# Pairs 0 to 5 of an attention stage: rotation on the vector engine, transposed weights copied out by the scalar engine

## The chip, the cores and the metric

The kernel runs on one core of a Trainium2 chip. The metric is the device time of one execution in microseconds (us), the median of several runs. PE is TensorE, DVE is VectorE, ACT is ScalarE, POOL is GpSimd, SP is the engine whose queue issues the DMA transfers.

## The reference

Rotary attention over 4 batches, 8 heads, 576 positions and 64 dimensions, then two feed-forward blocks over the 2304 tokens (model width 512, hidden width 2048), all in float32:

```python
q_rot, k_rot = rotate(q), rotate(k)     # x1*cos - x2*sin, x1*sin + x2*cos
scores = scale * q_rot @ k_rot.T
scores = scores - max(scores)
attn = exp(scores); attn = attn / (sum(attn) + 1e-9)
x = attn @ v                            # laid out as 2304 x 512
h = x @ w_in                            # first block
g = where(h >= 1, h, where(h <= -1, 0, (h + 1) ** 2 / 4))
x = g @ w_out
g = s * relu(x @ w_in2) ** 2 + b        # second block
out = g @ w_out2
```

## The kernel before, in words

Two heads are handled together as a pair: 16 pairs, i = 0 to 15. To keep float32 accuracy, operands are split into a high part in the float32r type and a low part (the rest), and products are summed from both.

The rotation of a pair's q or k is `rope_pair` (line 240 onwards). The tile holds q (or k) twice, as it is and with its halves swapped, 576 columns each. It is multiplied by the table of cosines and sines (1152 elements per partition, L246) and the two halves are added (576 elements, L248). Where GpSimd does it, `pool_tt` (L86) cuts an operation into pieces of at most 300 elements. For q, `lay_q` (L261, L262) writes high and low parts stacked for the matmuls. For k, `lay_k` copies the high part by the scalar engine (L272, tile `kin`), subtracts it to get the low part (576 elements), and spreads both by six DMA transfers (L277, L278) into `kh` and `kz`. For pair 0 all of this is done in halves on DVE ahead of the loop.

The scores of a pair are made in nine units, k = 0 to 8: eight of 128 rows of one head (four of head 0, four of head 1) and one, k = 4, of the 64 last rows of both heads. A unit is (`qk`): matmuls into one of two score buffers `sc` in PSUM (L305), the row maximum `nm` by DVE straight out of PSUM (L307), and exponential with row sums by ACT (L312) into the tile `p` in SBUF. The score buffer is free for the next unit but one when the exponential is done.

Two units later (`tmain`) PE transposes `p` in four blocks of 128x128 into a PSUM bank `tp` (L327), which is copied to `pt` in SBUF (512 elements per partition): units of head 0 by ACT (L331), unit 4 by ACT (L329), units of head 1 by DVE (L333). The last 64 columns are gathered and transposed after units 4 and 8 (`trem`) and copied to `ptr` by DVE (L344), 384 and 256 elements. After units 4 and 8, `inverse` takes reciprocals of the sums (L365, L367, L369 on DVE, L371 on POOL), and two units further `finish` multiplies the weights by v (`av`, L353), transposes the reciprocals (`rm`), copies them by ACT (L383) and scales the result by DVE (L386) into `u`, which goes to DRAM.

Beside the pairs, weights of the feed-forward blocks are loaded and converted from their 64-bit form (`Slice.half`): ACT L126, four steps on DVE (L127 to L130), ACT L131, two steps on POOL (L86, tiles `wm` and `w`). From pair 5 on, matmuls of the first block on the batches already finished fill PE (`beside`, matmuls at L144).

One loop over n (the number of the unit, 9 for each pair) calls, in the order "qltaf", the units' scores, the loads and rotations, the transposes, the products with v and the filling. The rotation of pair i + 1 is called in pair i, q at k = 0 and k at k = 2:

```python
if k == 0:
    rope_pair(i + 1, "q", nc.gpsimd if i else nc.vector, nc.vector, None)
elif k == 2:
    rope_pair(i + 1, "k", nc.gpsimd, nc.gpsimd, [nc.gpsimd, nc.vector])
```

So before, pair 1's q is multiplied by DVE and all later ones by GpSimd; all adds for q are on DVE; everything for k from pair 1 on is on GpSimd. A scheduler then sets the order on each engine; it takes rotations as early as buffers allow (four tiles for q and k together), up to two pairs ahead. Each engine runs its instructions strictly in that order.

After the attention, the rest of the first block and the second block run as dense matmuls (`stage`).

Of the kernel before, what the change touches and what calls it, by code (L numbers as in the profile page):

```python
# [14 lines left out]
ALU = mybir.AluOpType  # L15
# [8 lines left out]
P = 128  # L24
# [28 lines left out]
N2A = 288  # L53
CAV = None
BF = 0
SPLITX = 1
N1 = 288

# [2 lines left out]
def kernel(ctx, tc, qq, kk, vv, tab, ww1, ww2, s, b, out):  # L61
    nc = tc.nc
# [12 lines left out]
    def pool_tt(out, in0, in1, op, dim=-1):  # L75

        n = out.shape[dim]
        free = 1
        for x in out.shape[1:]:
            free *= x  # L80
        k = min(n, -(-free // PW))
        for i in range(k):
            c = [slice(None)] * len(out.shape)
            c[dim] = slice(n * i // k, n * (i + 1) // k)
            c = tuple(c)
            nc.gpsimd.tensor_tensor(out=out[c], in0=in0[c], in1=in1[c], op=op)  # L86
# [112 lines left out]
    ps_s = pp.enter_context(tc.tile_pool(name="ps_s", bufs=2, space=PSUM))  # L199
    ps_b = pp.enter_context(tc.tile_pool(name="ps_b", bufs=4 - BF, space=PSUM))  # L200
    ps_f = pp.enter_context(tc.tile_pool(name="ps_f", bufs=BF, space=PSUM)) if BF else ps_b

    tab_sb = att.tile([P, 2, S], F32, name="tab_sb")

    def bank(name):
        return ps_b.tile([P, 512], F32, tag="bank", name=name)
# [6 lines left out]
    def load_qk(i, nm, pieces=WHOLE):  # L213
        bb, hp = divmod(i, NP)
        t = att2.tile([P, 2, S], F32, tag="qkin", name=f"{nm}in", bufs=QB)
        for c in pieces:
            nc.sync.dma_start(out=t[:, :, c], in_=(qq if nm == "q" else kk)[bb, hp, :, :, c])
        qk_in[nm, i] = t

    def load_v(i):  # L220
        bb, hp = divmod(i, NP)
        t = att2.tile([P, 5, 2, D], F32, tag="vin", name="vin", bufs=VB)
        nc.sync.dma_start(out=t, in_=vv[bb, hp])
        v_in[i] = t
# [15 lines left out]
    def rope_pair(i, nm, mul, add, lo_eng, pieces=WHOLE):  # L240

        t = qk_in.pop((nm, i))
        tt = {nc.gpsimd: pool_tt, nc.vector: nc.vector.tensor_tensor}
        last = None
        for c in pieces:
            tt[mul](out=t[:, :, c], in0=t[:, :, c], in1=tab_sb[:, :, c], op=ALU.mult)  # L246
            r = t[:, 1, c]
            tt[add](out=r, in0=t[:, 0, c], in1=r, op=ALU.add)  # L248
            last = (lay_q if nm == "q" else lay_k)(i, t, c, lo_eng)
        return last  # L250
# [13 lines left out]
    def lay_k(i, t, c, lo_engs):  # L264
        if c.start == 0:
            stacks["k", i] = att.tile([P, 2, S], F32R, tag="kh", name="kh", bufs=2), kz_t[i % 2]
        kh, kz = stacks["k", i]
        tt = {nc.gpsimd: pool_tt, nc.vector: nc.vector.tensor_tensor}
        r = t[:, 1, c]
        if i > 0:  # L270
            hi, lo = t[:, 0, c].bitcast(F32R), r.bitcast(F32R)
            nc.scalar.copy(hi, r)  # L272
            pool_tt(out=lo, in0=r, in1=t[:, 0, c], op=ALU.subtract)
            for j in range(2):
                own = SELF[j]
                for rows in SELF:
                    nc.sync.dma_start(out=kh[rows, j, c].bitcast(F32), in_=t[own, 0, c])  # L277
                m = nc.sync.dma_start(out=kz[own, j, c].bitcast(F32), in_=t[own, 1, c])  # L278
            return m.ins
        for j in range(2):  # L280
            own, other = SELF[j], SELF[1 - j]
            nc.scalar.copy(kh[own, j, c], r[own])
            m = nc.sync.dma_start(out=kh[other, j, c].bitcast(F32), in_=kh[own, j, c].bitcast(F32))
            tt[lo_engs[j]](out=kz[own, j, c], in0=r[own], in1=kh[own, j, c], op=ALU.subtract)
        return m.ins
# [4 lines left out]
    pt = {}  # L290
# [25 lines left out]
    def tmain(i, k):  # L316
        j, t = UNITS[k]
        g, o = (0, 256) if j is None else divmod(t * P, 256)
        if k in (0, 5):
            n = GROUPS[g][1]  # L320
            pt[g] = att.tile([P, 4, 2, n], F32, tag="pt", name="pt", bufs=TB)
            pt["r", g] = att.tile([P, 384], F32, tag="ptr", name="ptr", bufs=TB)
        tp = bank("tp")
        v = tp.rearrange("p (c w) -> p c w", c=4)
        p = p_t[i, t][:, (S + D) * (j == 0):]
        for c in range(4):
            nc.tensor.transpose(v[:, c, :], p[:, c * P:(c + 1) * P], ident)  # L327
        if j is None:
            nc.scalar.copy(pt[g][:, :, :, o:o + D], tp.rearrange("p (c j w) -> p c j w", c=4, j=2))  # L329
        elif j == 0:  # L330
            nc.scalar.copy(pt[g][:, :, 0, o:o + P], v)  # L331
        else:
            nc.vector.tensor_copy(pt[g][:, :, 1, o:o + P], v)  # L333

    def trem(i, g):

        tp = bank("tr")
        for n in range(2):
            nc.tensor.transpose(tp[:, n * P:(n + 1) * P], p_t.pop((i, 2 * g + n))[:, 512:640], ident)
        m = 256  # L340
        if g == 0:
            nc.tensor.transpose(tp[:, 256:384], p_t.pop((i, 4))[:, 512:640], ident)
            m = 384
        nc.vector.tensor_copy(pt["r", g][:, :m], tp[:, :m])  # L344

    def av(i, g):

# [104 lines left out]
    def convert():  # L452
        while pending:
            sl = pending.pop(0)
            if sl.made < 2:
                sl.half(wst, WB)
                break
# [20 lines left out]
    def do_load(n):  # L478
        if n < len(units):
            i, k = units[n]  # L480
            if i + 1 < NPAIR:
                if k == 0:
                    rope_pair(i + 1, "q", nc.gpsimd if i else nc.vector, nc.vector, None)
                elif k == 2:
                    rope_pair(i + 1, "k", nc.gpsimd, nc.gpsimd, [nc.gpsimd, nc.vector])
                elif k == 3:
                    load_v(i + 1)
                elif k in (4, 6) and i + 2 < NPAIR:
                    load_qk(i + 2, "q" if k == 4 else "k")

        if n in range(33, 51, 2) or n in range(70, 110, 4):
            with tc.issue_after(exps[n - 14]):
                convert()

    def do_t(n):
        if LT <= n < len(units) + LT:
            i, k = units[n - LT]
            tmain(i, k)
            if k in (4, 8):
                trem(i, k // 8)  # L500
                rbs[i, k // 8] = inverse(i, k // 8)
# [9 lines left out]
    def do_fill(n):  # L511
        if n < 48:
            return
        with tc.issue_after(exps[min(n, len(units)) - 4]):
            run_fill(0.85 if n < 90 else 0.98)

    acts = {"q": do_qk, "l": do_load, "t": do_t, "a": do_av, "f": do_fill}
    for n in range(len(units) + LA):
        with ExitStack() as st:
# [156 lines left out]
```

## Time and profile before

| what | value |
|---|---|
| median of 3 runs | 1170.19 us |
| lowest and highest of them | 1165.18 and 1172.96 us |
| the profiled execution | 1167.95 us |
| its span, first to last instruction | 1166.2 us |
| mean granted TensorE clock | 0.988 |
| PE busy | 1104.3 us (95%) |
| DVE busy | 604.2 us (52%) |
| ACT busy | 692.6 us (59%) |
| POOL busy | 563.5 us (48%) |
| last product of the attention scaled (L386) | 462.2 us from the start |

The span begins with the first instruction; times in rows are counted from there. Busy shares are means over stages of different kinds: the attention with little else (to some 150 us), the attention with fillings (to 462 us), and the dense stages. PEclk is the clock granted to TensorE, 1.00 for full speed; a PE busy at a lower clock does less in the same time. In a row of the timeline the square brackets hold how long the engine was idle before it and what ended that.

### The profile page before, as it was taken

The page shows a single profiled execution, that of the slowest core. Times are in us where ns is not written, and L with a number is a line of the kernel's source. Part 1 is how long each engine was busy: PE and PEld are TensorE (multiplying, and loading weights), DVE is VectorE, ACT ScalarE, POOL GpSimd, SP SyncE. Part 2 cuts the span into 40 slices and gives each one's busy share as a digit, 9 for nine tenths or more (in the row PEclk, how much of TensorE's full clock was granted, in tenths as well). Part 3 has the DMA queues.
Part 4 walks back from the last instruction along what each step waited for, and adds up shares of the span by engine and source line. Part 5 has one row for each costly group of instructions (what it writes and reads, how often), then busy time and mean ns, then how long its engine had stood idle before and what let it go on. Part 6 is the DMA issues. An engine that isn't in the chain of part 4 may idle for free.

```text
span 1166.2 us, 18826 instructions
## 1 busy us (share of the span) xinstructions
PE 1104.3 (95%) x6816; PEld 997.2 (86%) x6816; DVE 604.2 (52%) x1030; ACT 692.6 (59%) x1450; POOL 563.5 (48%) x748
## 2 busy tenths in 40 slices
PE   4988799889999999999999889999999999999998
PEld 3666688778889988998999889998888889988887
DVE  6788888886565553566655566554411111221221
ACT  4666667756666655666555455567665555555443
POOL 6977797774441101766688886556610110111000
PEclk9988899999999999999999999999999999999999
DMA  7655555554443311434345453434211210312220
GB/s 230 185 163 154 155 160 172 175 160 123 124 120 97 91 40 58 142 124 135 102 147 157 146 166 132 131 122 145 94 38 60 66 40 26 98 39 70 66 65 33
DMA packets 68573, 132.63 MB, mean 114 GB/s; under 512 B 8448, under 2 KB 46592, under 8 KB 68480
## 3 DMA queue, kind: packets, MB, share of 16 engines
q1 hardware_dynamic: 68480, 131.43, 37.0%
q8 instruction: 53, 0.87, 0.3%
q14 instruction: 40, 0.33, 0.1%
HBM read 91.29 MB, written 26.54 MB: 101 GB/s over the span
## 4 chain that ended last, share of the span: by engine, by line
PE 69%; POOL 9%; DVE 8%; DMA 5%; issue 4%; ACT 4%; SPq 1%; POOLq 0%; ACTq 0%; DVEq 0%
PE hps L144 23%; PE yps L590 8%; PE yps L591 8%; PE yps L589 8%; PE sc L305 6%; PE h L144 4%; PE av L353 4%; PE y L144 4%; PE tp L327 3%; POOL w L86 2%; POOL wm L86 2%; DMA xs<-xd 2%; POOL xl L86 2%; DVE nm L307 1%; ACT p L312 1%
## 5 line engine op out<-in xcount | busy, mean ns | idle before, releaser
L144 PE MATMUL hps<-xh,w 128*128 128x464 f32 (+5 forms) x1216 | 344.4, 349 | 0.9 <-POOL w L86 0.9
L86 POOL TENSOR_TENSOR xl<-xs,xh 128x232 fp32r<-128x232 f32 (+5 forms) x172 | 132.3, 793 | 270.9 <-ACT xh L90 270.7
L144 PEld LDWEIGHTS hps<-xh,w 128*128 128x128 f32 x1216 | 221.7, 188 | 16.1 <-POOL w L86 1.1
L589 PE MATMUL yps<-gh,w 128*128 128x464 f32 (+5 forms) x608 | 213.3, 351 | 4.6 <-ACT yo L596 4.2
L590 PE MATMUL yps<-gl,w 128*128 128x464 f32 (+5 forms) x608 | 212.7, 350 | 5.1 <-DVE gl L94 5.1
L591 PE MATMUL yps<-gh,w 128*128 128x464 f32 (+5 forms) x608 | 212.5, 350 | 0.0
L144 PE MATMUL hps<-xl,w 128*128 128x464 f32 (+5 forms) x608 | 211.5, 348 | 0.4 <-POOL xl L86 0.4
L94 DVE TENSOR_TENSOR gl<-ar,gh 128x464 fp32r<-128x464 f32 (+1 forms) x80 | 56.7, 708 | 266.9 <-ACT gh L90 266.8
L86 POOL TENSOR_TENSOR wm<-wm,w 128x256 f32<-128x256 f32 x128 | 114.5, 914 | 119.7 <-ACT w L131 61.1
L305 PE MATMUL sc<-kh,qs 128*128 128x288 f32 (+2 forms) x384 | 110.7, 323 | 44.6 <-ACT p L312 31.3
L307 DVE TENSOR_REDUCE nm<-sc 128x1 f32<-128x576 f32 x144 | 107.4, 751 | 62.7 <-PE sc L305 62.4
L589 PEld LDWEIGHTS yps<-gh,w 128*128 128x128 f32 x608 | 114.5, 188 | 14.4 <-ACT yo L596 6.0
L590 PEld LDWEIGHTS yps<-gl,w 128*128 128x128 f32 x608 | 114.6, 189 | 13.5 <-DVE gl L94 6.0
L312 ACT ACTIVATE p<-sc,nm 128x576 f32<-128x576 f32 x144 | 106.7, 743 | 29.6 <-DVE nm L307 28.8
L175 ACT ACTIVATE ar<-hps 128x464 f32<-128x464 f32 (+1 forms) x80 | 44.3, 554 | 129.8 <-PE hps L144 129.8
L144 PEld LDWEIGHTS hps<-xl,w 128*128 128x128 f32 x608 | 114.2, 188 | 8.3 <-POOL xl L86 0.7
L591 PEld LDWEIGHTS yps<-gh,w 128*128 128x128 f32 x608 | 114.6, 189 | 7.5
L305 PEld LDWEIGHTS sc<-kh,qs 128*128 128x128 f32 x384 | 71.4, 198 | 53.3 <-ACT p L312 38.6
L305 PE MATMUL sc<-kz,qs 128*128 128x288 f32 (+2 forms) x384 | 100.6, 298 | 0.0
L86 POOL TENSOR_TENSOR w<-wm,wa 128x256 fp32r<-128x256 f32 x128 | 99.7, 795 | 0.1
L94 DVE TENSOR_TENSOR gl<-ac,gh 128x288 fp32r<-128x288 f32 (+3 forms) x112 | 78.0, 696 | 35.0 <-ACT gh L90 33.5
L327 PE MATMUL tp<-ident,p 128*128 128x128 f32 x576 | 90.4, 281 | 0.0
(81 smaller groups left out, 1991.3 us busy)
## 6 DMA issues: line engine op xcount, KB each, us to landing
wraw<-in_ww SPq DMA_DIRECT2D x64, 512.0 KB, 3.8
kin<-in_k SPq DMA_DIRECT2D x15, 576.0 KB, 4.6
qin<-in_q SPq DMA_DIRECT2D x15, 576.0 KB, 4.0
kh<-kin SPq DMA_DIRECT2D x60, 144.0 KB, 2.6
xs<-y1d SPq DMA_DIRECT2D x32, 232.0 KB, 2.5
xs<-xd SPq DMA_DIRECT2D x44, 144.0 KB, 2.3
yd<-ys SPq DMA_DIRECT2D x40, 144.0 KB, 2.2
vin<-in_v SPq DMA_DIRECT2D x16, 320.0 KB, 3.0
```

Source lines behind the costliest of these rows:

```text
L86: nc.gpsimd.tensor_tensor(out=out[c], in0=in0[c], in1=in1[c], op=op)
L94: tt(out=dst_lo, in0=src, in1=dst_hi, op=ALU.subtract)
L144: m = nc.tensor.matmul(out_ps, l, r, start=(i == 0), stop=(i == n - 1))
L175: nc.scalar.activation(r, h, AF.Relu)
L305: nc.tensor.matmul(sc[:, half, o:o + n], l, r[:, k0:k0 + n], start=m == 0, stop=m == len(todo) - 1)
L307: nc.vector.tensor_reduce(out=nm, in_=sc[:, :, :288], axis=AX.XY, op=ALU.max, negate=True)
L312: exps[i * 9 + k] = nc.scalar.activation(p, sc[:, :, :288], AF.Exp, bias=nm, scale=1.0, accum_out=sums_t[i][:, col:col + 1]).ins
L327: nc.tensor.transpose(v[:, c, :], p[:, c * P:(c + 1) * P], ident)
L353: nc.tensor.matmul(ps[j * D:(j + 1) * D, :n], v[:, kt, j, :], pt[g][:, kt, j, :], start=kt == 0, stop=False)
L589: nc.tensor.matmul(acc, wh, gh, start=f == 0, stop=False)
L590: nc.tensor.matmul(acc, wh, gl, start=False, stop=False)
L591: nc.tensor.matmul(acc, wl, gh, start=False, stop=last)
```

## The change

A new constant NB = 6 sets how many pairs count as first. For pairs 1 to 5 the whole rotation goes to DVE: the multiplications and the adds of q and k, and the subtraction that gives k's low part. For pairs 0 to 5 the copies of transposed weights that DVE did (L333 and L344) go to ACT. From pair 6 on all is as before.

```diff
+NB = 6
...
             hi, lo = t[:, 0, c].bitcast(F32R), r.bitcast(F32R)
             nc.scalar.copy(hi, r)
-            pool_tt(out=lo, in0=r, in1=t[:, 0, c], op=ALU.subtract)
+            tt[lo_engs[0]](out=lo, in0=r, in1=t[:, 0, c], op=ALU.subtract)
...
         elif j == 0:
             nc.scalar.copy(pt[g][:, :, 0, o:o + P], v)
+        elif i < NB:
+            nc.scalar.copy(pt[g][:, :, 1, o:o + P], v)
         else:
             nc.vector.tensor_copy(pt[g][:, :, 1, o:o + P], v)
...
-        nc.vector.tensor_copy(pt["r", g][:, :m], tp[:, :m])
+        if i < NB:
+            nc.scalar.copy(pt["r", g][:, :m], tp[:, :m])
+        else:
+            nc.vector.tensor_copy(pt["r", g][:, :m], tp[:, :m])
...
                 if k == 0:
-                    rope_pair(i + 1, "q", nc.gpsimd if i else nc.vector, nc.vector, None)
+                    rope_pair(i + 1, "q", nc.vector if i < NB - 1 else nc.gpsimd, nc.vector, None)
                 elif k == 2:
-                    rope_pair(i + 1, "k", nc.gpsimd, nc.gpsimd, [nc.gpsimd, nc.vector])
+                    e = nc.vector if i < NB - 1 else nc.gpsimd
+                    rope_pair(i + 1, "k", e, e, [e, e])
```

The scheduler orders anew. In the changed kernel the line numbers are one to seven higher (L246 is L247, L248 is L249, L307 is L308, L312 is L313, the new copies by ACT are L334 and L348). On PE the order of pairs 0 to 5 is nearly the same. Three places on the other engines:

DVE at the start of pair 0, from the first maximum on, before (`nm` is a maximum, the products with `tab_sb` and the adds are rotations of pair 1 and pair 2):

```order
L307 TENSOR_REDUCE nm<-sc 128x1 x2
L246 TENSOR_TENSOR qin<-qin,tab_sb 128x1152
L307 TENSOR_REDUCE nm<-sc 128x1
L248 TENSOR_TENSOR qin<-qin 128x576
L307 TENSOR_REDUCE nm<-sc 128x1
L333 COPY pt<-tp 128x4x128
L262 SCALAR_TENSOR_TENSOR qs_103<-qin,qs_103 64x576 x2
L307 TENSOR_REDUCE nm<-sc 128x1
L365 TENSOR_SCALAR sume<-sums 128x4
L307 TENSOR_REDUCE nm<-sc 128x1
L248 TENSOR_TENSOR qin<-qin 128x576
L333 COPY pt<-tp 128x4x128
```

And now:

```order
L308 TENSOR_REDUCE nm<-sc 128x1
L247 TENSOR_TENSOR kin<-kin,tab_sb 128x1152
L308 TENSOR_REDUCE nm<-sc 128x1
L249 TENSOR_TENSOR kin<-kin 128x576
L247 TENSOR_TENSOR qin<-qin,tab_sb 128x1152
L308 TENSOR_REDUCE nm<-sc 128x1
L274 TENSOR_TENSOR kin<-kin 128x576
L249 TENSOR_TENSOR qin<-qin 128x576
L308 TENSOR_REDUCE nm<-sc 128x1
L247 TENSOR_TENSOR qin<-qin,tab_sb 128x1152
L263 SCALAR_TENSOR_TENSOR qs_103<-qin,qs_103 64x576
L247 TENSOR_TENSOR kin<-kin,tab_sb 128x1152
```

Five rotations' steps more stand between the first four maxima, and two whole multiplications follow behind the fourth; the copy into `pt` is gone.

DVE in pair 3, from the maximum of unit 3 to those of units 4 and 5, before (`wm` and `wa` are weight conversion):

```order
L307 TENSOR_REDUCE nm<-sc 128x1
L128 SCALAR_TENSOR_TENSOR wm<-wa,wm 128x512
L333 COPY pt<-tp 128x4x128
L129 TENSOR_SCALAR wa<-wm 128x512
L365 TENSOR_SCALAR sume<-sums 128x4
L248 TENSOR_TENSOR qin<-qin 128x576
L130 SCALAR_TENSOR_TENSOR wa<-wraw,wa 128x512
L386 TENSOR_TENSOR u<-av,r 128x256
L307 TENSOR_REDUCE nm<-sc 128x1 x2
```

And now (`L249` is the add for pair 6's q):

```order
L308 TENSOR_REDUCE nm<-sc 128x1
L129 SCALAR_TENSOR_TENSOR wm<-wa,wm 128x512
L130 TENSOR_SCALAR wa<-wm 128x512
L249 TENSOR_TENSOR qin<-qin 128x576
L131 SCALAR_TENSOR_TENSOR wa<-wraw,wa 128x512
L371 TENSOR_SCALAR sume<-sums 128x4
L392 TENSOR_TENSOR u<-av,r 128x256
L308 TENSOR_REDUCE nm<-sc 128x1 x2
```

The copy into `pt` is gone, the rest stands between the same maxima.

ACT in pair 3, around the exponential of unit 4, before (`r` are the reciprocals):

```order
L131 CAST w<-wm 128x512
L383 COPY r<-rm 128x256
L331 COPY pt<-tp 128x4x128
L312 ACTIVATE p,sums<-sc,nm 128x576
L314 COPY p<-p 128x64
L329 COPY pt<-tp 128x8x64
L312 ACTIVATE p,sums<-sc,nm 128x576 x2
```

And now:

```order
L132 CAST w<-wm 128x512
L389 COPY r<-rm 128x256
L332 COPY pt<-tp 128x4x128
L313 ACTIVATE p,sums<-sc,nm 128x576
L334 COPY pt<-tp 128x4x128
L315 COPY p<-p 128x64
L330 COPY pt<-tp 128x8x64
L313 ACTIVATE p,sums<-sc,nm 128x576
L348 COPY ptr<-tr 128x384
L313 ACTIVATE p,sums<-sc,nm 128x576
```

One copy into `pt` stands between the exponentials of units 4 and 5 in addition, and the copy into `ptr` between those of units 5 and 6.

POOL, in the changed kernel, has between its work on pair 0's k and the multiplication for pair 6's q only the small operations (`vin`, `eb`) and the weight conversion.

## Rows read from the trace of the kernel before

**Rows 1.** The page, first line: span of the profiled execution

```profile
span 1166.2 us, 18826 instructions
```

**Rows 2.** Windows, pairs 0 to 5 and the stretch behind them; columns in the first line

```profile
core 0: us, PE busy (x) PEld busy (x) DVE busy (x) ACT busy (x) POOL busy (x), PEclk, DMA share, GB/s
13.30:38.20 24.90, 20.13 (x120) 16.74 (x121) 19.21 (x32) 14.32 (x32) 21.24 (x28) 0.93 0.79 262
38.20:57.00 18.80, 16.70 (x132) 13.08 (x131) 15.09 (x26) 13.03 (x29) 18.29 (x25) 1.00 0.62 167
57.00:82.50 25.50, 21.19 (x148) 17.03 (x147) 20.27 (x39) 15.56 (x36) 17.85 (x24) 0.87 0.52 148
82.50:106.30 23.80, 20.29 (x140) 16.08 (x139) 18.40 (x34) 15.07 (x34) 16.79 (x25) 0.86 0.57 167
106.30:130.90 24.60, 20.61 (x143) 16.39 (x142) 19.80 (x36) 16.01 (x35) 18.36 (x26) 0.86 0.54 157
130.90:155.00 24.10, 20.65 (x156) 16.46 (x155) 21.55 (x36) 16.12 (x39) 22.63 (x29) 1.00 0.61 183
155.00:270.00 115.00, 105.06 (x812) 90.36 (x811) 95.81 (x165) 79.27 (x191) 87.93 (x111) 1.00 0.52 161
```

**Rows 3.** Timeline of PE in pair 3, the two waits

```profile
93.61 0.40 PE L305 MATMUL sc<-kh,qs 128*128 128x288 f32 x1 [1.65 <-ACT p L312]
...
96.25 0.77 PE L305 MATMUL sc<-kh,qs 128*128 128x64 f32 x2 [1.08 <-ACT p L312]
```

**Rows 4.** Timeline of DVE in pair 3, between two maxima

```profile
87.46 0.68 DVE L128 SCALAR_TENSOR_TENSOR wm<-wa,wm 128x512 uint32<-128x512 uint32 x1
...
89.68 0.74 DVE L248 TENSOR_TENSOR qin<-qin 128x576 f32<-128x576 f32 x1
90.35 1.28 DVE L130 SCALAR_TENSOR_TENSOR wa<-wraw,wa 128x512 f32<-128x512 uint16 x1
...
91.88 1.41 DVE L307 TENSOR_REDUCE nm<-sc 128x1 f32<-128x576 f32 x2
```

**Rows 5.** Timeline of ACT in pair 3, behind those maxima

```profile
92.72 0.74 ACT L312 ACTIVATE p<-sc,nm 128x576 f32<-128x576 f32 x1 [1.30 <-DVE nm L307]
...
94.88 0.59 ACT L329 COPY pt<-tp 128x512 f32<-128x512 f32 x1 [1.05 <-PE tp L327]
```

**Rows 6.** Lines by form, DVE, 15 to 155 us; line engine op names shapes xcount | busy, mean ns | idle before

```profile
L333 DVE COPY pt<-tp 128x512 f32<-128x512 f32 x23 | 15.7, 682 | 0.2
...
L248 DVE TENSOR_TENSOR qin<-qin 128x576 f32<-128x576 f32 x8 | 8.6, 1070 | 1.6 <-POOL qin L86 1.5
...
L344 DVE COPY ptr<-tr 128x384 f32<-128x384 f32 x6 | 3.2, 530 | 0.0
...
L246 DVE TENSOR_TENSOR qin<-qin,tab_sb 128x1152 f32<-128x1152 f32 x1 | 1.5, 1481 | 0.7 <-DMA qin<-in_q 0.7
```

**Rows 7.** Lines by form, DVE, 0 to 25 us

```profile
L248 DVE TENSOR_TENSOR kin<-kin 128x288 f32<-128x288 f32 x2 | 0.9, 452 | 0.0
...
L248 DVE TENSOR_TENSOR qin<-qin 128x576 f32<-128x576 f32 x1 | 0.7, 744 | 0.0
```

**Rows 8.** Lines by form, ACT, 13.3 to 155 us

```profile
L331 ACT COPY pt<-tp 128x512 f32<-128x512 f32 x23 | 13.4, 584 | 8.8 <-PE tp L327 8.6
...
L383 ACT COPY r<-rm 128x384 f32<-128x384 f32 x6 | 2.9, 478 | 7.8 <-PE rm L380 7.8
```

**Rows 9.** Lines by form, POOL, 15 to 165 us

```profile
L86 POOL TENSOR_TENSOR kin<-kin,tab_sb 128x288 f32<-128x288 f32 x36 | 36.8, 1051 | 3.7 <-DMA kin<-in_k 3.7
L86 POOL TENSOR_TENSOR qin<-qin,tab_sb 128x288 f32<-128x288 f32 x32 | 26.9, 869 | 2.4 <-DMA qin<-in_q 2.4
L86 POOL TENSOR_TENSOR kin<-kin 128x288 f32<-128x288 f32 x17 | 15.4, 912 | 0.2
L86 POOL TENSOR_TENSOR kin<-kin 128x288 fp32r<-128x288 f32 x16 | 14.6, 932 | 0.7 <-ACT kin L272 0.6
```

**Rows 10.** Timeline of POOL in pair 0: arrival of pair 2's q

```profile
23.96 3.07 POOL L86 TENSOR_TENSOR qin<-qin,tab_sb 128x288 f32<-128x288 f32 x4 [0.56 <-DMA qin<-in_q]
```

## Prediction

> **What bounds the kernel now.** I read the windows first, cut at the first row maximum (nm, L307) of each pair. [rows 2] show the stretch that the change touches: pairs 0 to 5, from 13.3 to 155 us. Pair 1 takes 18.80 us at full clock; pairs 2 to 5, which also convert weights, take 25.50, 23.80, 24.60 and 24.10. No engine is full: in pair 3 PE is busy 20.29 of 23.80 us, DVE 18.40, ACT 15.07, POOL 16.79. So it is a chain through several engines that sets the pace: scores on PE, maximum on DVE, exponential on ACT, which frees one of two score buffers for PE. The granted clock says the same: 0.87, 0.86 and 0.86 in pairs 2 to 4. [...]
>
> Next the timelines of one such pair. In pair 3 PE waits 1.65 us and then 1.08 us for an exponential [rows 3]; the matmuls behind the second wait are the slow ones (0.77 us for the two short ones). The exponential had waited 1.30 us for a maximum [rows 5], and DVE had been busy without a hole since 87.46 us: conversion steps, a copy of transposed weights, sums, the add of q's rotation, and only at 91.88 the next two maxima [rows 4]. That bunch of 4.4 us between maxima is the bound. Behind it ACT runs the exponential of unit 4 and then waits 1.05 us for transposes before a copy [rows 5]; the next exponential stands behind that copy. POOL's rotations are a second limit: DVE's adds waited 1.5 us for them [rows 6]. Behind 155 us, PE is busy 105.06 of 115.00 us at full clock [rows 2]; there it has its own work, and a gain or loss ahead of it should move the rest of the span unchanged.
>
> **The change, part by part.** Counts come from the code and the order of instructions.
>
> POOL loses 16 pieces of q's multiplication (pairs 2 to 5) at 0.869 us, 20 of k's (pairs 1 to 5) at 1.051, ten adds at 0.912 and ten subtractions at 0.932 [rows 9]: 13.9 + 21.0 + 9.1 + 9.3 = 53.3 us, nearly all of it in pairs 0 to 2, because rotations run ahead. It goes on rotating pairs 6 and later from pair 3 on, as before.
>
> DVE gains nine whole multiplications of 1152 elements, five adds and five subtractions of 576. An add runs 0.744 us undisturbed [rows 7]; I take this for the subtraction too. The one whole multiplication in the trace took 1.481 us, beside a busy POOL [rows 6]: the upper end. The lower end is from the adds: 0.452 us for 288 and 0.744 for 576 elements [rows 7], thus 0.292 for each further 288, and 0.744 + 2 x 0.292 = 1.33 us. I take 1.33, since POOL will be nearly idle there. On DVE that makes 9 x 1.33 + 10 x 0.744 = 19.4 us (20.8 by the upper end). It loses 24 copies of 0.682 and 12 remainder copies of at most 0.530 [rows 6]: 22.7 us. So DVE is level in sum; what changes is where its work stands.
>
> Rows first: the same add took 1.070 us in the mean while POOL rotated [rows 6], against 0.744 [rows 7]. [...]
>
> ACT gains 24 copies of 0.584 us and 12 remainder copies, for which its own copies of the same size out of PSUM stand, 0.478 us [rows 8]: 14.0 + 5.7 = 19.7 us in 141.7, from 90.1 us busy (the sum of ACT in the six pairs of rows 2) to 109.8, 77%.
>
> Now by pair, because only the chain counts.
>
> Pair 0. By the order DVE does six whole multiplications before pair 1's first maximum instead of one, six adds instead of two, three subtractions, and four copies fewer: 5 x 1.33 + 4 x 0.744 + 3 x 0.744 - 3 x 0.682 - 0.530 = 9.3 us more. It is idle 24.90 - 19.21 = 5.7 us there [rows 2]. If all of that is filled the pair ends 3.6 us later, less some 0.6 for adds no longer stretched: +3.0. If nothing is filled, +9. Pair 2's q arrives at 23.96 us at the earliest [rows 10], and DVE now waits for it itself with maxima behind; it will be there at about 23.7 us by my sum, so I charge nothing, but up to 1 us if the load is late. That k is laid out earlier brings nothing, as pair 1 did not wait for it.
>
> Pair 1. DVE: 2 x 1.33 + 0.744 - 4 x 0.682 - 2 x 0.530 = -0.4 us; ACT +3.3 us on 13.03 of 18.80. Cost 0 (-1 to +1.5).
>
> Pair 2. DVE +0.35 us, by the same count with one add more. It took 1.7 us longer than pair 3 at much the same work [rows 2], and the wait of DVE for POOL's q product lies in such places (1.5 us in all) [rows 6]. That wait goes: -1.7. What is late next is the conversion on DVE, as in pair 3. Bounds: +0.4, and -5.5 if the pair comes down to 20 us.
>
> Pairs 3 to 5. DVE loses 3.8 us each and ACT gains 3.3. But the bunch loses only its one copy: 0.7 of 4.4 us; the add, the four conversion steps and the sums stay together, and POOL works beside them as before. On ACT a copy of 0.584 now stands between the exponential of unit 4 and the one of unit 5, and a remainder copy of 0.478 before that of unit 6. The first lies partly within the 1.05 us in which ACT waited. I take -0.7 for each pair, together -2.1; ends are +1.1 for each (both copies bare) and -5 (the 3.3 us of clock and half of the waits gone too).
>
> Behind 155 us the order differs for two or three pairs and is then the same again; no row gives a sign: 0, within 3 us.
>
> Sum: 3.0 + 0 - 1.7 - 2.1 = -0.8 us. The profiled execution took 1167.95 us, 1166.2 of span [rows 1] and 1.75 around it, so 1167.2. It lies 2.2 us below the median of the three runs (1165.18 to 1172.96), so I name 1168.
>
> **The rivals.**
>
> [...]
>
> Rival B, slower: the scalar engine takes the place of the vector engine. It works strictly in order, so a copy whose transposes are not ready holds the exponentials behind it; this trace has 8.6 us of such waits at L331 already [rows 8]. [...] It decides as soon as ACT's exponentials start later than their maximum is ready in most units. Against: 77% busy, and ACT idles 1 us or more at several places of each pair.
>
> Rival C, within the forecast's range: work moved between GpSimd and DVE is simply neutral, so the rotations change nothing and only the copies count: 1168 less 0 to 3 us. [...]
>
> **How the numbers follow.** A measurement of this kernel can tell about 1%, 11.7 us, from no change. No change by that mark (my sum and rival C): 0.57. Rival A reaching 1% and beyond: 0.27. Rival B: 0.16. The range goes from rival A with its first waits gone, 1151, to a little beyond rival B, 1182; it leaves out cases in which several unknown ends fall together. The forecast's own range is 1159 to 1176.
>
> **What would show it.** Right: pair 1's first maximum some 3 us later than 38.2 us, pair 2 shorter by about 2, pairs 3 and 4 still with a clock near 0.86 and a DVE bunch of 3.5 us or more ahead of unit 4's maximum; nine multiplications of about 1.33 us. [...] Wrong towards B: ACT above 85% in a pair, with maxima ready long before their exponentials. Wrong altogether: a change behind 155 us larger than that ahead of it.

## The result and the profile after

The change takes 1182.45 us (median of five runs, 1176.91 to 1185.33) where the kernel before took 1170.19 in runs beside it (1165.18 to 1174.22): ratio 1.0102, interval 1.0071 to 1.0133. Measured again later it gave 1186.25 us and 1.0113 (1.0081 to 1.0146). It is slower by 1.0 to 1.1%, some 12 to 15 us; the forecast was 1168, and 1182 the upper end of its range. The profiled execution of after took 1182.45 us, the median itself, with this span and these engines:

```profile
span 1180.7 us, 18794 instructions
...
PE 1112.4 (94%) x6816; PEld 1004.7 (85%) x6816; DVE 602.8 (51%) x1013; ACT 707.8 (60%) x1486; POOL 510.7 (43%) x692
```

POOL gave up what was counted: it was busy 563.5 us before and is 510.7 now, 52.8 less (53.3 forecast). ACT went from 692.6 to 707.8, 15.2 more (19.7 forecast), DVE from 604.2 to 602.8, 1.4 less (3.3 forecast). On both, rows that stand back to back overlap by some 0.1 us, which the counts left out (in after, DVE's multiplication at 25.87 lasts 1.36 us and the next row begins at 27.15; ACT's copy at 100.45 lasts 0.58 us and the next row begins at 100.92). The windows of after, cut at each pair's first maximum as in [rows 2], pairs 0 to 6:

```profile
core 0: us, PE busy (x) PEld busy (x) DVE busy (x) ACT busy (x) POOL busy (x), PEclk, DMA share, GB/s
13.20:43.80 30.60, 23.40 (x126) 19.39 (x126) 25.93 (x40) 17.36 (x37) 1.39 (x6) 0.89 0.78 248
43.80:65.00 21.20, 18.13 (x132) 14.51 (x133) 14.86 (x26) 14.99 (x35) 1.10 (x4) 0.92 0.37 106
65.00:89.80 24.80, 21.54 (x147) 17.27 (x145) 19.66 (x33) 17.84 (x40) 6.43 (x11) 0.86 0.49 148
89.80:110.60 20.80, 16.95 (x134) 13.50 (x134) 15.79 (x30) 16.87 (x39) 15.16 (x23) 1.00 0.59 171
110.60:135.20 24.60, 20.05 (x139) 15.87 (x138) 16.40 (x29) 17.46 (x40) 17.90 (x25) 0.86 0.58 172
135.20:159.10 23.90, 20.47 (x164) 17.07 (x163) 18.81 (x29) 18.74 (x43) 21.37 (x27) 1.00 0.58 171
159.10:194.20 35.10, 30.19 (x220) 25.38 (x219) 26.15 (x46) 24.07 (x59) 24.97 (x33) 0.95 0.51 153
```

The same window of pair 6 in the kernel before:

```profile
155.00:185.50 30.50, 29.43 (x226) 25.21 (x225) 25.84 (x48) 22.73 (x56) 24.66 (x32) 1.00 0.54 166
```

The table has the time from a pair's first maximum to the next pair's, read from the DVE timelines of the two profiles (the last line: first maximum of pair 0 to that of pair 6).

| pair | before, us | after, us | difference |
|---|---|---|---|
| 0 | 23.1 | 28.9 | +5.8 |
| 1 | 18.8 | 21.2 | +2.4 |
| 2 | 25.5 | 24.9 | -0.7 |
| 3, 4, 5 | 23.8, 24.6, 24.2 | 20.7, 24.6, 24.0 | -3.1, 0, -0.2 |
| 6 | 30.4 | 35.1 | +4.7 |
| 7, 8 | 28.5, 25.6 | 28.8, 26.6 | +0.2, +0.9 |
| 9 | 32.8 | 34.8 | +2.0 |
| 0 to 5 | 140.0 | 144.2 | +4.2 |

Of the 14.5 us by which the span is longer, 4.2 lie ahead of pair 6, 7.8 in pairs 6 to 9, the rest behind. All pair times here and below are of one execution of each kernel; a second one of the change took 148.3 us for pairs 0 to 5. The order of the instructions differs from before's only up to the end of pair 7 (some 213 us in before, 223 in after). So the 2.0 us of pair 9 and the 2.5 behind it need another reason: kernels further down that have before's order there take 34.5 to 36.7 us for pair 9 as well, and the stretch behind pair 9 takes 892 to 897 us in every kernel with four tiles for q and k (before 893.7, after 896.3).

**Pair 0.** DVE is busy 6.7 us more (25.93 against 19.21) and the window is 5.7 longer: DVE's idle time went only from 5.69 to 4.67 us. But it is idle for another reason. Between the first maximum of pair 0 and that of pair 1, before it waited for the scalar engine, scores, a load and POOL; now it waits for no score, and 3.5 us go to loads of q and k. DVE's waits in that stretch, before, then after:

```profile
DVE u L386 <- ACT r L383: 2.1, 1, 2.1
DVE nm L307 <- PE sc L305: 1.0, 2, 0.8
DVE qin L246 <- DMA qin<-in_q: 0.7, 1, 0.7
DVE qin L248 <- POOL qin L86: 0.7, 1, 0.7
...
```

```profile
DVE qin L247 <- DMA qin<-in_q: 3.3, 2, 2.1
DVE kin L274 <- ACT kin L273: 0.4, 1, 0.4
DVE kin L247 <- DMA kin<-in_k: 0.2, 1, 0.2
```

(The three numbers are us in total, times, and the longest.) POOL has almost nothing to do, and DVE's timeline shows what stands between the maxima (L308):

```profile
23.70 1.36 DVE L247 TENSOR_TENSOR qin<-qin,tab_sb 128x1152 f32<-128x1152 f32 x1 [1.24 <-DMA qin<-in_q]
25.09 0.75 DVE L263 SCALAR_TENSOR_TENSOR qs<-qin,qs 64x576 fp32r<-64x576 f32 x1
25.87 1.36 DVE L247 TENSOR_TENSOR kin<-kin,tab_sb 128x1152 f32<-128x1152 f32 x1
27.15 0.75 DVE L308 TENSOR_REDUCE nm<-sc 128x1 f32<-128x576 f32 x1
...
33.79 1.36 DVE L247 TENSOR_TENSOR qin<-qin,tab_sb 128x1152 f32<-128x1152 f32 x1 [2.08 <-DMA qin<-in_q]
35.06 0.75 DVE L274 TENSOR_TENSOR kin<-kin 128x576 fp32r<-128x576 f32 x1
35.73 0.75 DVE L249 TENSOR_TENSOR qin<-qin 128x576 f32<-128x576 f32 x1
36.40 0.75 DVE L308 TENSOR_REDUCE nm<-sc 128x1 f32<-128x576 f32 x1
```

The multiplications at 23.70 and 25.87 belong to pair 2, those at 33.79 and 37.07 to pair 3. All ten of pairs 1 to 5 begin between 15.82 and 70.02 us: the rotations run up to three pairs ahead, not two, and each stands in a queue that the maxima must pass. The one at 33.79 waited 2.08 us for a q that SP could issue only at 28.71, as its tile came free with the layout at 27.93. For the maximum at 27.15 TensorE waited the longest in this pair:

```profile
28.82 0.47 PE L306 MATMUL sc<-kh,qs 128*128 128x288 f32 x1 [3.28 <-ACT p L313]
```

**Pair 6.** Nothing was edited there, but the scheduler's order is another. ACT in after, a conversion step (L127) and the two exponentials behind it, then TensorE's wait for the first of them:

```profile
181.51 0.66 ACT L127 ACTIVATE wa<-wraw 128x512 f32<-128x512 f32 x1 [3.90 <-POOL w L87]
...
183.65 0.75 ACT L313 ACTIVATE p<-sc,nm 128x576 f32<-128x576 f32 x1
...
184.38 0.74 ACT L313 ACTIVATE p<-sc,nm 128x576 f32<-128x576 f32 x1
```

```profile
184.54 0.48 PE L306 MATMUL sc<-kh,qs 128*128 128x64 f32 x2 [2.84 <-ACT p L313]
```

ACT in the kernel before, at the same place:

```profile
176.51 0.75 ACT L312 ACTIVATE p<-sc,nm 128x576 f32<-128x576 f32 x1
...
177.23 0.75 ACT L312 ACTIVATE p<-sc,nm 128x576 f32<-128x576 f32 x1
...
179.58 0.69 ACT L126 ACTIVATE wa<-wraw 128x512 f32<-128x512 f32 x1 [0.47 <-POOL w L86]
```

Before, the exponentials went first. In after they stand behind the conversion, which waits 3.90 us for POOL, though their maxima were taken at 176.79 and 178.26. TensorE then waits 2.84 us, and the granted clock of the window is 0.95 instead of 1.00.

### The profile page after: what moved, and what is told of

Same layout as the page of the kernel before. It is cut to its first block, busy times and chain, and to the rows that moved or that the text cites. A ratio compares the mean times of both kernels' runs of the same rounds, so it can differ in the third digit from the quotient of the medians.

```text
span 1180.7 us, 18794 instructions
## 1 busy us (share of the span) xinstructions
PE 1112.4 (94%) x6816; PEld 1004.7 (85%) x6816; DVE 602.8 (51%) x1013; ACT 707.8 (60%) x1486; POOL 510.7 (43%) x692
## 4 chain that ended last, share of the span: by engine, by line
PE 67%; POOL 8%; DVE 8%; DMA 7%; ACT 5%; issue 4%; SPq 1%; POOLq 0%; ACTq 0%; DVEq 0%
PE hps L145 23%; PE yps L597 8%; PE yps L598 8%; PE yps L596 8%; PE sc L306 5%; PE h L145 4%; PE y L145 4%; PE av L359 3%; PE tp L328 3%; POOL wm L87 2%; POOL w L87 2%; DMA xs<-xd 2%; DMA kin<-in_k 2%; POOL xl L87 2%; ACT p L313 2%
## 5 line engine op out<-in xcount | busy, mean ns | idle before, releaser
L306 PE MATMUL sc<-kh,qs 128*128 128x288 f32 (+2 forms) x384 | 113.7, 330 | 51.0 <-ACT p L313 37.6
L308 DVE TENSOR_REDUCE nm<-sc 128x1 f32<-128x576 f32 x144 | 107.8, 753 | 64.7 <-PE sc L306 64.1
L313 ACT ACTIVATE p<-sc,nm 128x576 f32<-128x576 f32 x144 | 107.2, 746 | 31.4 <-DVE nm L308 30.6
L597 PEld LDWEIGHTS yps<-gl,w 128*128 128x128 f32 x608 | 115.0, 189 | 12.3 <-DVE gl L95 4.7
L328 PE MATMUL tp<-ident,p 128*128 128x128 f32 x576 | 92.9, 286 | 0.0
```

The lines of the kernel that those rows point to most:

```text
L306: nc.tensor.matmul(sc[:, half, o:o + n], l, r[:, k0:k0 + n], start=m == 0, stop=m == len(todo) - 1)
L308: nc.vector.tensor_reduce(out=nm, in_=sc[:, :, :288], axis=AX.XY, op=ALU.max, negate=True)
L313: exps[i * 9 + k] = nc.scalar.activation(p, sc[:, :, :288], AF.Exp, bias=nm, scale=1.0, accum_out=sums_t[i][:, col:col + 1]).ins
L597: nc.tensor.matmul(acc, wh, gl, start=False, stop=False)
```

## The experiments

**One part alone.** The rotation without the copies, against the kernel before:

```diff
+NB = 6
...
-            pool_tt(out=lo, in0=r, in1=t[:, 0, c], op=ALU.subtract)
+            tt[lo_engs[0]](out=lo, in0=r, in1=t[:, 0, c], op=ALU.subtract)
...
-                    rope_pair(i + 1, "q", nc.gpsimd if i else nc.vector, nc.vector, None)
+                    rope_pair(i + 1, "q", nc.vector if i < NB - 1 else nc.gpsimd, nc.vector, None)
...
-                    rope_pair(i + 1, "k", nc.gpsimd, nc.gpsimd, [nc.gpsimd, nc.vector])
+                    e = nc.vector if i < NB - 1 else nc.gpsimd
+                    rope_pair(i + 1, "k", e, e, [e, e])
```

> Rotation on DVE for pairs 1 to 5, all copies as before. Theory 1 (the loss comes from rotations and transfer waits of DVE ahead of maxima in pairs 0 and 1, and from one inverted order on ACT in pair 6): pair 1's first maximum at 42 us or later (before 38.2, change 43.8), pairs 2 to 5 together no shorter than before (98 us), total 1176 to 1184. Theory 2 (the copies on ACT are the load that slows): pair 0 may be longer, but the total is within 1167 to 1173.

Measured: 1186.17 us, ratio 1.0129 (1.0077 to 1.0181). Pair 0 takes 30.0 us, and pair 6 begins at 166.8 instead of 155.1 (in the slowest of its four executions). The time is a little above theory 1's range. The rotation alone, with the other order that it brings behind pair 5, is enough for the whole loss.

The copies without the rotation, against the kernel before:

```diff
+NB = 6
...
+        elif i < NB:
+            nc.scalar.copy(pt[g][:, :, 1, o:o + P], v)
...
-        nc.vector.tensor_copy(pt["r", g][:, :m], tp[:, :m])
+        if i < NB:
+            nc.scalar.copy(pt["r", g][:, :m], tp[:, :m])
+        else:
+            nc.vector.tensor_copy(pt["r", g][:, :m], tp[:, :m])
```

> Copies of pairs 0 to 5 on ACT, rotation on GpSimd as before. Theory 1: pair 1's first maximum within 1 us of 38.2, pairs 2 to 5 together 3 to 6 us shorter than the 98 us of before, total 1162 to 1168 unless the order of pair 6 is inverted there too. Theory 2: ACT's copies hold its exponentials, pairs 1 to 5 longer by 1 to 2 us each, total 1176 or more.

Measured: 1176.01 us, ratio 1.0038 (1.0021 to 1.0056). Pairs 0 to 5 are level with before (pair 6 begins at 154.6), with ACT busy 17.5 instead of 15.1 us in pair 3; pairs 6 and 9 take 34.6 and 36.7 us, and the loss is there. ACT waits 3.93 us at 176.45 for POOL's w, as in after: the case that theory 1 had left open. The time is at theory 2's bound, but pairs 1 to 5 are not longer, as theory 2 had them.

**The rotation held back.** The change with the rotation of pairs 2 to 5 allowed only behind the last maximum of the pair two before (q) and the second maximum of the pair before (k):

```diff
+HQ = 8
+HK = 10
...
+                        if 1 <= i < NB - 1:
+                            hold.enter_context(tc.issue_after(maxima[9 * i - 9 + HQ]))
...
```

> The change, but DVE's rotation of pairs 2 to 5 is ordered behind maxima of the pair before, so that it no longer runs up to two pairs ahead; DVE does the same work. Theory 1: pair 1's first maximum at 38 to 40 us and pair 2's before 61 (change 43.8 and 65.0), and 4 to 7 us less in total than the change: 1173 to 1179. Theory 2 (or DVE's sheer load as the cause): the same work costs the same, 1180 to 1185.

Measured: 1180.90 us, ratio 1.0089 (1.0055 to 1.0123). The loss of pair 0 is gone, 20.5 us, and pair 3 begins at 78.7, 3.8 earlier than before. Then pairs 3 and 4 take 27.0 and 29.1 us (48.4 together in before). Their windows:

```profile
78.70:105.70 27.00, 20.34 (x140) 15.96 (x139) 24.28 (x37) 19.19 (x43) 17.96 (x22) 0.87 0.48 140
105.70:134.80 29.10, 23.63 (x132) 18.52 (x133) 23.73 (x38) 17.63 (x39) 24.43 (x30) 0.71 0.68 186
```

The rotations of pairs 4 and 5 now meet the weight conversion, on a DVE that is busy 24.28 of 27.00 us; TensorE waits 4.45 and 2.91 us in pair 4 and its clock falls to 0.71. Theory 1 was right on pairs 0 and 1; the time is theory 2's, as the work that hurt in pair 0 hurts here.

**One inversion of pair 6 undone.** The change, with the conversion of n = 70 issued behind a later exponential:

```diff
-            with tc.issue_after(exps[n - 14]):
+            with tc.issue_after(exps[n - (10 if n == 70 else 14)]):
```

> The change, with one weight conversion ordered behind the exponential of unit 6 of pair 6, as the order of before had it. Theory 1: pairs 0 to 5 as in the change, pair 6 about 30 to 32 us instead of 35, total 1177 to 1180. If the loss behind 155 us has another cause: pair 6 stays at 34 us or more, total 1181 to 1185.

Measured: 1187.33 us, ratio 1.0144 (1.0109 to 1.0179). Pair 6 takes 33.0 us, 2.1 less, but pair 7 30.4, 1.6 more. The time is above both theories. With this one place mended, ACT waits 3.29 us for an output tile (ys) ahead of two exponentials of pair 6. The run doesn't show whether the order as a whole is the cause.

**The whole order as before.** Where the copies are moved in some of pairs 0 to 3 alone, the scheduler returns by pair 4 to the order of the kernel before, on all engines; with none moved, as in the rotation alone, it does so only at the end of pair 7. So the whole rotation could be measured with that order behind it:

```diff
+NC = 4
...
-        elif i < NB:
+        elif i < NC:
             nc.scalar.copy(pt[g][:, :, 1, o:o + P], v)
...
-        if i < NB:
+        if i < NC:
             nc.scalar.copy(pt["r", g][:, :m], tp[:, :m])
```

> The whole rotation as in the change, the two copies on the scalar engine only in pairs 0 to 3; every engine then has, from some point in pair 4 on, the same instructions in the same order as the kernel before. Theory (what the change loses behind pair 5 it loses because the work of pairs 6 to 9 stands in another order): pair 6 begins near 159 us (4 later than before), takes 30.4 us again and pair 9 near 33, and the time is near 1174.5 us, about 4 above before. Rival 1 (the delay of the first pairs carries on by itself, whatever the order): pair 6 takes about 35 us and the time stays near 1182. Rival 2 (the two copies of pairs 4 and 5 are what the vector engine needs to be rid of): pairs 4 and 5 take 2 us more each and the time is above 1182.

Measured: 1179.86 us, ratio 1.0064 (1.0039 to 1.0089). Pair 6 takes 30.5 us, and pairs 6 to 8 84.6, as before (after: 90.4). The time lies between theory and rival 1, since pairs 0 to 5 of this profile took 9.0 us more than in before, not 4.

The same with the copies alone, pairs 0 to 3:

> Only the copies moved, and only in pairs 0 to 3; the order from pair 4 on is that of before. Theory (order): the 1.0038 of the run with the copies of six pairs goes, time within 1.5 us of before, pair 6 takes 30.4 us again. Rival (the scalar engine's added copies cost by themselves): near 1174, pair 6 above 33 us.

Measured: 1172.73 us, ratio 1.0013 (0.9995 to 1.0030), pair 6 30.3 us. The copies cost nothing that can be told once the order behind them is the old one.

To price the order, the change ran once more beside two kernels that have its whole rotation and the old order from pair 4 on (NC = 3 and NC = 1).

> The change itself, for comparison with the next two on the same chip. Both theories: near 1182 us; in a second profile pair 0 again 28 to 30 us and pair 6 again near 35 us. That pair 3 took only 20.8 us in the first profile may or may not come again.

> Whole rotation as in the change, copies on the scalar engine in pairs 0 to 2 only; from pair 4 on the order of before. Theory (the other order of pairs 6 to 9 costs some 4 us): pair 6 takes 30.3 to 30.6 us and the time is 3 to 5 us below the change beside it. Rival (the order costs nothing in the time, what pair 6 gains is lost elsewhere): time within 1.5 us of the change.

> Whole rotation as in the change, copies on the scalar engine in pair 0 only; from pair 4 on the order of before. Theory (order): pair 6 takes 30.3 to 30.6 us, time 3 to 5 us below the change beside it, and as the run with three pairs. Rival (the moved copies of pairs 1 to 3 were worth something): 1 to 3 us above the run with three pairs.

Measured: change 1186.25 (1.0113, 1.0081 to 1.0146), three pairs 1178.45 (1.0050, 1.0029 to 1.0071), one pair 1179.34 (1.0056, 1.0032 to 1.0079). The change's pair 6 takes 34.7 us again, and its conversion waits as long as in the first profile:

```profile
184.85 0.66 ACT L127 ACTIVATE wa<-wraw 128x512 f32<-128x512 f32 x1 [3.93 <-POOL w L87]
```

With the old order pair 6 takes 30.3 and 29.9 us. The two medians lie 7.8 and 6.9 us below the change's, more than was expected, and the number of copies makes no difference that can be told. In this round the order is about half of the loss. Other comparisons price it lower, each time against before of the same round: the change loses 12.3 us and the kernel with NC = 4 8.2; the copies of six pairs lose 5.0 us and those of four pairs 1.1. The rotation alone, in the other order, loses 15.2 us, with one pair's copies and the old order 8.0. So the order costs 4 to 8 us, a third to a half. The 6 to 8 us that the kernels with the old order still lose are the rotation in pairs 0 to 3.

**Work or waits?** In pair 0 DVE has both more work and waits for q. A fifth tile for raw q and k (QB = 5) is to let the loads begin earlier; first in the kernel before, as a control:

```diff
-QB = 4
+QB = 5
```

> The kernel before with a fifth tile for the raw q and k of a pair (QB = 5 instead of 4): from pair 2 on each load of q or k is free to start one layout earlier. It is the control for the next two runs. All theories: pair 0 about 23 us as before, time within 5 us of before either way, since the scheduler's order behind pair 5 moves with it.

Measured: 1168.08 us, ratio 0.9964 (0.9940 to 0.9987), the lowest ratio of all kernels here. Pair 0 takes 22.7 us, pairs 2 and 4 21.7 and 21.5, pair 6 33.1.

Then the same line in the kernel with NC = 4:

> The whole rotation on the vector engine, the two copies on the scalar engine in pairs 0 to 3, and the fifth tile; from pair 6 on the order of the instructions of the scalar and vector engines is that of the control. Theory (what pairs 0 to 2 lose is the vector engine's waiting for q and k with maxima queued behind): no wait of the vector engine for a q or k transfer above 0.5 us in pairs 0 and 1, pair 0 near 24 us instead of 29 to 30, pairs 0 to 2 together within 2 us of the control, time within 3 us of the control. Rival (the loss is the vector engine's added work itself, 1.36 us for a multiplication and 0.75 for an addition, ahead of the maxima): waits gone but pair 0 still above 27 us, pairs 0 to 2 at least 6 us above the control, time 6 to 9 above it.

Measured: 1188.30 us, ratio 1.0150 (1.0106 to 1.0194). Pair 0 takes 31.3 us, and pairs 0 to 2 79.5 (control 64.4). The tile let the scheduler run the rotation still further ahead: seven multiplications instead of six stand in pair 0, and DVE is busy 27.61 of 33.00 us (its window, the first fence). Pair 3's q is now multiplied without a wait (its timeline, the second), but other loads are waited for (the third).

```profile
13.30:46.30 33.00, 25.64 (x126) 21.24 (x126) 27.61 (x41) 18.37 (x39) 1.32 (x5) 0.84 0.80 248
```

```profile
29.88 1.35 DVE L248 TENSOR_TENSOR qin<-qin,tab_sb 128x1152 f32<-128x1152 f32 x1
31.14 0.75 DVE L309 TENSOR_REDUCE nm<-sc 128x1 f32<-128x576 f32 x1
```

```profile
24.11 1.36 DVE L248 TENSOR_TENSOR qin<-qin,tab_sb 128x1152 f32<-128x1152 f32 x1 [1.31 <-DMA qin<-in_q]
...
36.40 1.36 DVE L248 TENSOR_TENSOR kin<-kin,tab_sb 128x1152 f32<-128x1152 f32 x1 [1.72 <-DMA kin<-in_k]
...
39.65 1.36 DVE L248 TENSOR_TENSOR qin<-qin,tab_sb 128x1152 f32<-128x1152 f32 x1 [1.22 <-issue]
```

The last row names no releaser; SP issued that load only at 35.35. So the waits did not go, which both theories had as their condition, and the run doesn't decide between them. What it adds is one more multiplication and one more addition ahead of pair 1's first maximum: between the first maxima of pairs 0 and 1 DVE is busy 26.3 us against 24.6 with four tiles.

And the line in the change itself:

> The whole change with the fifth tile. By the theory of the waits its pairs 0 to 5 take what those of the run before take, and what it loses beyond that run is the other order of pairs 6 to 8: pair 6 again 3 to 5 us above the control, time 2 to 5 us above the run before. Rival (the order of pairs 6 to 8 costs nothing): same time as the run before within 1.5 us.

Measured: 1189.36 us, ratio 1.0129 (1.0095 to 1.0163). Pair 6 takes 33.9 us against 31.3 in the run before, but both times are alike. Here the order of pairs 6 to 8 gave nothing that can be told; its price holds for four tiles.

What separates work and waits in pair 0 are five profiles with four tiles. In them DVE has the same 36 instructions in the same order between the first maxima of pairs 0 and 1, and its only waits there are for loads of q and k, beside 0.45 us for a copy by ACT:

| kernel | pair 0, us | DVE busy, us | waits for q and k, us | pair 0 without them, us |
|---|---|---|---|---|
| one pair's copies (NC = 1) | 28.0 | 24.6 | 2.5 | 25.5 |
| change | 28.9 | 24.6 | 3.5 | 25.4 |
| NC = 4 | 29.8 | 24.6 | 4.4 | 25.4 |
| NC = 3 | 30.6 | 24.6 | 5.2 | 25.4 |
| change, second profile | 30.7 | 24.6 | 5.3 | 25.4 |

The pair grows by what DVE waits, us for us. Without the waits it takes 25.4 us, 2.3 more than before's 23.1 (which holds 0.7 of such a wait): that is DVE's added work, less what of it fills DVE's former idle time. The waits add 2.5 to 5.3.

**A better place for the rotation.** Only pairs 1 to 3, held as above, copies of pairs 0 to 2 (NB = 4, NC = 3 in the held kernel), order as before from pair 4 on; then the same for pairs 1 and 2 (NB = 3, NC = 2). Against the held kernel:

```diff
-NB = 6
+NB = 4
+NC = 3
...
-        elif i < NB:
+        elif i < NC:
```

> Rotation of pairs 1 to 3 on the vector engine and held behind maxima 8 and 10 of the pair before (as in the held run), copies of pairs 0 to 2 on the scalar engine, the rest and the order from pair 4 on as before. Theory: pairs 0 to 2 take about 63.5 us (before 67.4), pair 3 and those behind it take what they took before, and the time is 2 to 4 us below before, near 1167. Rival (an early start of pair 3 is given back there, because what it then waits for, loads or conversions, comes when it came before): pairs 3 and 4 together 2 to 4 us longer than before's 48.4, time within 1 us of before.

Measured: 1170.81 us, ratio 0.9994 (0.9973 to 1.0016). Pair 0 takes 20.3 us and pair 4 begins 3.0 us earlier than in before, but pair 1 takes 21.8 instead of 18.8, pair 9 34.6 instead of 32.8. The time is the rival's, but pairs 3 and 4 (47.1 us) are not longer than before's 48.4. All of the loss is gone, and no gain is left that the times show. (The profile is of the fastest of the twelve executions, 1166.57 us.)

> As the run with three held rotations, with the rotation of pairs 1 and 2 and the copies of pairs 0 and 1 alone. Theory: pairs 0 and 1 take about 40.6 us (before 41.9), the rest as before, time 1 to 3 us below before. Rival: given back in pair 2, which then waits for its own transfers; time within 1 us of before.

Measured: 1181.23 us, ratio 1.0074 (1.0044 to 1.0103): both theories wrong, pairs 0 and 1 take 48.8 us. Pair 3's q is POOL's again, arrives late, and DVE's add for it stands with q's layout (2.49 us) ahead of the first maxima of pair 1. DVE, then TensorE:

```profile
37.46 1.33 DVE L253 TENSOR_TENSOR qin<-qin 128x576 f32<-128x576 f32 x1 [4.62 <-POOL qin L90]
38.82 2.49 DVE L267 SCALAR_TENSOR_TENSOR qs<-qin,qs 64x576 fp32r<-64x576 f32 x2
41.24 0.74 DVE L312 TENSOR_REDUCE nm<-sc 128x1 f32<-128x576 f32 x1
```

```profile
42.96 0.77 PE L310 MATMUL sc<-kh,qs 128*128 128x64 f32 x2 [6.99 <-ACT p L317]
```

One add that waits 4.62 us, with the layout behind it, makes TensorE wait 6.99 us, because maxima are queued behind both. The last run put the held rotation into the kernel with the fifth tile (NB = 4, NC = 2, QB = 5):

> Fifth tile for the raw q and k; rotation of pairs 1 to 3 on the vector engine, held behind maxima 8 and 10 of the pair before; copies of pairs 0 and 1 on the scalar engine; from pair 4 on the order is that of the control with the fifth tile (1168.1 us, profiled: pairs 0 to 3 together 87.95 us). Theory (the rotation costs the vector engine nothing once it stands behind the maxima, and frees GpSimd): no wait of TensorE above 3 us in pairs 0 to 3, these four at least 1 us below the control's 87.95, time 1164 to 1168. Rival (the rotation on the vector engine is no gain even at its best place): pairs 0 to 3 at or above 88 us, time 1168 to 1173.

Measured: 1175.43 us, ratio 1.0052 (1.0032 to 1.0072); pairs 0 to 3 take 97.0 us, against the control's 87.95, and the time is above both theories. Pair 0 is short (20.2 us), but pair 1 takes 30.1: an add of DVE waits 4.24 us for POOL's q ahead of two maxima, as with the two held rotations.

```profile
43.23 1.33 DVE L253 TENSOR_TENSOR qin<-qin 128x576 f32<-128x576 f32 x1 [4.24 <-POOL qin L90]
```

The rotation on DVE gained nothing at any place that was tried.

## Why the prediction was wrong

The forecast of no change is on the wrong side of its 1% mark, and what was to show it "wrong altogether" came: +10.3 us behind pair 5, +4.2 ahead of it, against 0 and -0.8 (in the second profile of the change +9.9 and +8.3).

- **The step that failed most: "Behind 155 us ... 0, within 3 us".** The order of two or three pairs was seen to differ, and was priced at nothing because no row gave it a sign and PE "has its own work" there (105.06 of 115.00 us busy) [rows 2]. That share says nothing about in-order queues: PE is idle 4.9 us in pair 6 (35.10 - 30.19) where it had been 1.1, and 2.84 of them are one wait for exponentials set behind a conversion step. By the kernels with the old order, the order costs 4 to 8 us; of the 10.3, pair 9 and the stretch behind it (4.5) are not part of that. The order itself was there to be read: the conversion ahead of two exponentials. What each of its inversions costs stays open, as undoing this one didn't win the time back.
- **Pair 0: +3.0, measured +5.8.** The durations were right: multiplications 1.36 us (1.33 forecast), adds and subtractions 0.75. DVE's added work, 6.7 us, was even below the 8.7 that was summed (9.3 less 0.6). The fill came about for the most part: of the 5.3 us that DVE was idle between the two first maxima, 4.5 are filled once the waits for loads are left out, and the pair is then 2.3 us longer. That this is near +3.0 is partly luck, as work and fill both came out smaller. The term that failed is the transfers, "I charge nothing, but up to 1 us if the load is late": q came at 23.7 as forecast, yet DVE had then waited 1.24 us, and 2.08 more for pair 3's q, which the sum had not looked at; with 0.16 for k that makes 3.5 us, and 2.5 to 5.3 in the other profiles.
- **Pair 1: 0 (-1 to +1.5), measured +2.4.** TensorE waits 2.39 us for this pair's first exponential, where it waited 0.76, and 3.7 us for exponentials in all, where it was 2.1; the clock is 0.92 where it was 1.00. That the rotations cause this by standing ahead of the maxima is likely, but no run shows it for this pair alone.
- **Pair 2: -1.7, measured -0.7; pairs 3 to 5: -2.1, measured -3.3.** Sign and size are right. The second profile of the change has 70.9 us for pairs 3 to 5 against 72.6 before, -1.6, so the single profile's 20.7 us of pair 3 was partly luck: its clock was 1.00, in the second profile 0.93. The end of -5 for each of these pairs counts 3.3 us of clock; no run shows this term by itself. What the profiles show is TensorE at a granted clock of 0.50 for 6.70 us of pair 3 in before (from 95.75 to 102.45) and at 1.00 in the whole pair in after, which is 3.1 us shorter though TensorE waits 3.8 us for exponentials there, 3.5 before; pair 4 kept 0.86 and its 24.6 us.
- **Rival A**, a time lower by 1% or more (0.27), did not come: pairs 2 and 4 kept a clock of 0.86, and no kernel here shows a time near the range's lower end, 1151 (the lowest median is 1168.08). **Rival B** had the direction, and the range's upper end, 1182, put a little beyond it, is near the measured 1182.45; but it had not the cause: ACT is at most 81% busy in a pair ahead of pair 6 (16.87 of 20.80), and the copies alone cost nothing with the old order. **Rival C**, moved work is neutral, holds for the held kernel with three rotations (0.9994), not for the change, where the queue decides.

What stays open is how work and waits share what pairs 1 to 3 lose, as only pair 0 could be split. Nor was it tried to fix the order behind pair 5 by hand for the change.

## What to carry to other kernels

Work taken from an idle engine onto the engine that feeds a chain was paid here where it stood in that engine's queue: pair 0, with 6.7 us more work on DVE and 3.5 us of waits for loads, took 5.8 us longer, though DVE in sum was level (602.8 us busy against 604.2). So count what lies between the links of the chain, not the engine's sum, and ask which loads this engine now waits for itself. Idle time in which it used to wait for the chain could be filled (4.5 of 5.3 us in pair 0); a wait for a load ahead of the chain's next link was added whole (2.5 to 5.3 us in the five profiles of pair 0). A scheduler may move such work far ahead, here up to three pairs, and one instruction that waits for a load or another engine then stops the links behind it: with two held rotations one add that waited 4.62 us, with the layout behind it, made TensorE wait 6.99. Where an edit changes the order in a stretch that it doesn't touch, read that order for waiting instructions ahead of the chain's, and keep a kernel with the old order as a control: here the order alone was a third to a half of the result.

## What the runs showed of the hardware

In before and after, a DVE addition of 576 elements took 0.74 to 0.76 us or 1.18 to 1.36, and the longer times came only in rows beside a busy POOL. In after, ten of them from 17.77 to 72.97 us, beside which POOL has no step of rotation or conversion, took 0.75 or 0.76 us. In before, POOL is at such a step beside each of the 15: twelve took 1.18 to 1.36 us, and three 0.74 to 0.76 (at 19.56, 38.96 and 89.68). The one at 19.56 is the 0.744 of [rows 7], so that row was short, but not without POOL. In the held run, an addition of pair 2, and one of pair 4 beside POOL's subtraction for k (from 110.98, 2.07 us):

```profile
52.78 0.75 DVE L252 TENSOR_TENSOR qin<-qin 128x576 f32<-128x576 f32 x1
...
109.04 1.38 DVE L250 TENSOR_TENSOR kin<-kin,tab_sb 128x1152 f32<-128x1152 f32 x1
...
111.01 1.38 DVE L252 TENSOR_TENSOR kin<-kin 128x576 f32<-128x576 f32 x1
```

The add is stretched 1.8 times (1.38 against 0.75). The multiplication of twice the size is stretched less: it took 1.35 or 1.36 us in the ten rows of after up to 70.02, with POOL at no such step, 1.38 here (POOL at weight conversion from 108.48, 2.53 us) and 1.48 in before [rows 6] (POOL at k's multiplication from 16.22, 4.74 us). A busy POOL alone thus doesn't decide how long an addition takes; what else does, no run here shows.
